# Zero fill moved from the front part into the experts, five warm-up transposes fewer, and maxima stored ahead of the due step

## The chip, the core and the metric

The kernel runs on one NeuronCore of a Trainium2 chip. Five engines work side by side, each through its own list of instructions in order: TensorE (PE in the profile; its weight loads are shown apart as PEld), VectorE (DVE), ScalarE (ACT), GpSimd (POOL) and SyncE (SP), which here issues most of the transfers (DMAs). Engines wait for one another through semaphores. PE reads SBUF and writes PSUM; PSUM has eight banks of 128 x 512 float32 values. The metric is the device time of one execution in microseconds, the median of several runs.

## The reference

A row of 2048 tokens with 448 features goes through two blocks, and a sigmoid gate mixes their outputs:

```python
g = sigmoid((x * gate_w).sum(-1, keepdims=True))
# A: attention, 16 heads of 28, no mask
q, k, v = split_heads(x @ wqkv)
p = softmax(q @ k.T * 28 ** -0.5)
a = merge_heads(p @ v) @ wo
# B: 8 experts of width 1792, the two best per token
logits = x @ w_gate
topk_idx = argsort(-logits)[:, :2]
gates = softmax(take_along_axis(logits, topk_idx))
for e in range(8):
    w = (gates * (topk_idx == e)).sum(-1, keepdims=True)
    b += w * (silu(x @ w1[e]) @ w2[e])
out = g * a + (1 - g) * b
```

Everything is float32. Outside attention's last products the kernel gets float32 accuracy by splitting each operand into a high part and a remainder, so that one product becomes two or three matmuls.

## The kernel before, in words

**Front part (lines 238 to 617).** First come `BUSY` transposes of an identity on PE (`pt<-ident`, L339), which produce nothing that is used. Then a loop over 16 blocks of 128 tokens makes the values `v`, the router's logits and the gate (`v_block`, L334). ACT copies the values of each block from PSUM into a tile `v_s` (L376, three buffers), DVE copies the logits (L377), and SP stores `v_s` to DRAM (`v_d`, L382). DVE and ACT split the next tokens and the q/k weights meanwhile. Then follow seven tiles of q and k for all tokens (`qk_tile`, L569). Between their matmuls DVE works through `routing()`, which finds each token's two experts and its slot; its first PE step is a matmul on the finished masks `mb` (L431), which depends on the logits of all 16 blocks.

Every expert has 640 slots in the DRAM tensor `ys_d`, of which up to 576 are filled, and 24 blocks of 128 slots stand behind them for tokens that do not fit. Slots that no expert writes must hold zeros. In the kernel before, SP stores them from the SBUF tile `zf` in the token loop, from block 4 on: 24 stores at L385 and 8 at L388, each 128 x 448 values.

**Experts (lines 672 to 950).** Each of 8 experts is worked in two halves of its width (`hf` 0 and 1); I number the 16 halves 0 to 15. A half first makes the hidden values: 7 pieces, each 2 x 11 matmuls of 288 columns, 154 in all (L870; called U matmuls). Then the second product: one small part for slots 513 to 576 under `tc.If(cnt > 512)` (`last_slots`, L800), then four blocks of 128 slots with 21 matmuls of 448 columns each, 84 in all (L920; Y matmuls). Two PSUM banks, `acc0` and `acc1`, serve U and Y in turn. In the second half of an expert the next expert's tokens are transposed in between (L722; these halves are called `turns` in the code).

**The stream of maxima (`max_stream`, L91).** The softmax of attention needs the largest score of each query, and these are found beside the experts. A cell is one product of 128 queries and 512 keys for one head (L106); there are 1024. A step issues six cells into the six banks `pm`, or seven, the first into the idle `acc` bank (`spare`), when that bank is free. DVE then reduces each cell to its maxima: the cell in `acc` at L120, the others at L126 in two instructions, and at L135 it folds 16 partial maxima into the tile `mg`. 64 cells make one unit (a group of four heads and 512 queries). With a unit's last cell, its `mg` is appended to the list `flush`. `store_max` (L141) takes one `mg`, transposes it on PE into the idle `acc` bank (L142), copies it on DVE (`mr`, L144) and stores it (`m_d`, L145).

**When a step or a store is issued.** The program calls `worked` after every U and Y matmul; the order of PE's instructions is fixed by it at build time, not on the chip. `w1_due` and `W2_DUE` list after which U or Y matmul a step becomes due (one more is due at the start of the Y matmuls). At a due place, `worked` issues a store if `flush` holds one and the idle bank may be used, and puts the step off for `STORE_NS` of PE work (three Y matmuls); otherwise it issues the step. The idle bank may be used between the due place and three matmuls behind it (`free`, L923).

The instructions of SP are ordered by the framework's scheduler, not by hand: it may issue a transfer far ahead of the place in the program where it is written, as soon as its data are there.

Of the kernel before, what the change touches and what calls it, by code (L numbers as in the profile page):

```python
# [8 lines left out]
F32 = mybir.dt.float32  # L9
# [8 lines left out]

NXT = 8
A_AT = (1, 4)  # L20
BUSY = 20
STORE_NS = 600
U_NS, Y_NS, YT_NS = 131, 206, 452

S, D, H, DH, E, FF = 2048, 448, 16, 28, 8, 1792
# [4 lines left out]
CPAD = 640  # L30
NMAIN = E * CPAD
# [18 lines left out]
def tile_gated_mha_moe(ctx: ExitStack, tc: tile.TileContext, x, xT, wv, wqk, wo, w1, w2, out):  # L50
    nc = tc.nc
# [3 lines left out]
    dram = ctx.enter_context(tc.tile_pool(name="dram", bufs=1, space=DRAM))  # L55
# [6 lines left out]
    sum_d = dram.tile([NG * 4, 4, 512], F32, name="sum_d")  # L62
    idx_d = dram.tile([128, NSP], I32, name="idx_d")
    ys_d = dram.tile([NS, D], F32, name="ys_d")

    ident = consts.tile([128, 128], F32, name="ident")
    coef = consts.tile([128, 3, NT], F32, name="coef")
# [73 lines left out]
    def store_max(g, qc, mg, bank):  # L141
        nc.tensor.transpose(bank[0:16, 0:128], mg.rearrange("p j t -> p (j t)"), ident)  # L142
        mr = mxp.tile([16, 128], F32R, name="mr")
        nc.vector.tensor_copy(mr, bank[0:16, 0:128])  # L144
        nc.sync.dma_start(m_d[4 * g + qc].rearrange("h (t q) -> (h t) q", q=128), mr.bitcast(F32))  # L145
        done.append((g, qc))

    flush = []
# [7 lines left out]
    def tail_twice(xt):  # L156
        nc.scalar.activation(xt[:, D:512], xt[:, 384:D], AF.Copy)
# [15 lines left out]
    want, hold = [0], [0]  # L173
# [10 lines left out]
    def worked(ns, due=False, bank=None):  # L184
        hold[0] = max(0, hold[0] - ns)
        want[0] += due
        if want[0] and not hold[0]:
            if flush and bank:
                store_max(*flush.pop(0), bank())
                hold[0] = STORE_NS  # L190
                return
            if bank:
                spare.append(bank())
            next(ms, None)
            want[0] -= 1
            spare.clear()
# [41 lines left out]
    with ExitStack() as pa:  # L238
# [65 lines left out]
        nc.gpsimd.dma_start(neg_d.rearrange("o (a n) -> o a n", a=4), bc(neg.unsqueeze(1), [1, 4, 512]))  # L304
        zf = sb.tile([128, D], F32, name="zf")
        nc.gpsimd.memset(zf, 0.0)
        sbase = sb.tile([128, E + 1], F32, name="sbase")
        nc.gpsimd.memset(sbase[:, 0:1], 0.0)
        mb = sb.tile([128, NT + 1, E], BF, name="mb")
# [45 lines left out]
        for t in range(NT):  # L355
            ts = slice(t * 128, (t + 1) * 128)
            if t != 1:
                for t_ in ((0, 1) if t == 0 else (t,)):
                    pvs[t_] = ps.tile([128, 512], F32, name="pq")[:, 0:NV]

                for t_, j in (((0, 0), (0, 1), (1, 0), (1, 1), (0, 2), (1, 2), (0, 3), (1, 3)) if t == 0 else
                              [(t, j) for j in range(4)]):
                    v_block(t_, j)
            pv = pvs.pop(t)
            if 0 < t and t + 2 < NT:
                split_xt(t + 2)
            if 4 <= t < 12:
                b, c = divmod(t - 4, 2)
                cs = slice(c * D, (c + 1) * D)
                nc.scalar.activation(wqk_h[:, b, cs], wqr[t - 4], AF.Copy)  # L370
                nc.vector.tensor_tensor(wqk_l[:, b, cs], wqr[t - 4], wqk_h[:, b, cs].bitcast(F32),
                                        op=ALU.subtract)
            v_s = wk.tile([128, H, 32], F32, name="v_s")
            nc.gpsimd.memset(v_s[:, :, DH:DH + 1], 1.0)
            nc.gpsimd.memset(v_s[:, :, DH + 1:32], 0.0)
            nc.scalar.activation(v_s[:, :, 0:DH], pv[:, 0:D].rearrange("p (h d) -> p h d", h=H), AF.Copy)  # L376
            nc.vector.tensor_copy(lg[:, t], pv[:, D:D + E + 1])  # L377
            if t + NXT - 1 < NT:
                load_x(t + NXT - 1)
            if t < 8:  # L380
                load_wq(t)
            nc.sync.dma_start(v_d[ts], v_s.rearrange("p h d -> p (h d)"))  # L382
            if t >= 4:
                for i in range(2 * t - 8, 2 * t - 6):
                    nc.sync.dma_start(ys_d[NMAIN + i * 128:NMAIN + (i + 1) * 128], zf)  # L385
                    if i % 3 == 0:
                        r0 = (i // 3 + 1) * CPAD
                        nc.sync.dma_start(ys_d[r0 - CPAD + 512:r0], zf)  # L388

        def tmp(name, shape, dt=F32):  # L390
            return sb.tile(shape, dt, name=name)
# [280 lines left out]
    with ExitStack() as pb:  # L672
# [45 lines left out]
        def turn_x(xg, k, xeh, xel):  # L718
            n = CT[k]
            pt = ps.tile([128, 512], F32, name=f"acc{turn[0] ^ 1}").rearrange("p (b n) -> p b n", b=4)  # L720
            for b in range(4):
                nc.tensor.transpose(pt[:, b, :n], xg[:n, b * 128:(b + 1) * 128], ident[:n, :n])  # L722
            h, l = xeh[:, :, k * 128:k * 128 + n], xel[:, :, k * 128:k * 128 + n]
            f = xf[:, k % 4].rearrange("p (b n) -> p b n", b=4)[:, :, :n]
            nc.scalar.activation(h, pt[:, :, :n], AF.Copy)
            nc.scalar.activation(f, pt[:, :, :n], AF.Copy)
            nc.gpsimd.tensor_tensor(l, f[:, 0:3], h[:, 0:3].bitcast(F32), op=ALU.subtract)
            nc.gpsimd.tensor_tensor(h[64:128, 3], f[64:128, 3], h[64:128, 3].bitcast(F32), op=ALU.subtract)
# [100 lines left out]
        w1_due = [(18, 46, 73, 100, 128), (11, 35, 59, 83, 107, 131)]  # L829


        W2_DUE = [(15, 13, 12, 10), (16, 14, 13, 12)]

        for e in range(E):
            cnt = nc.values_load(cnt_i[0:1, e:e + 1], min_val=0, max_val=S)
# [6 lines left out]
            for hf in range(2):  # L842
# [53 lines left out]
                for n_k, k in enumerate((4, 0, 1, 2, 3)):  # L896
                    if k == 4:
                        if hf == 0:
                            ysb[4] = sb.tile([128, D], F32, name="ysb", bufs=5)
                        if (e, hf) == (E - 1, 1):  # L900
                            spilled()

                            nc.scalar.activation(sb.tile([128, 1], F32, name="warm", bufs=1), ident[:, 0:1], AF.Exp)
                        with tc.If(cnt > 512):
                            last_slots(e, hf, hs, ysb[4])
                        worked(0, True)
                        for f in range(NH):
                            fetch_w2(base + f + 9)
                    n = CT[k]
                    cs = slice(k * 128, k * 128 + n)  # L910
                    turns = hf == 1 and e + 1 < E
                    due = W2_DUE[turns][n_k - 1]
                    if k < 4:
                        py = accumulator()
                    i = 0
                    for f in range(NH if k < 4 else 0):
                        hh, hl, ht = hs[f]
                        w2h, w2l, w2r = w2t[base + f]
                        for a, b in ((hh, w2h), (hh, w2l), (hl, w2h)):
                            nc.tensor.matmul(py[:n, 0:D], a[:, cs], b, start=i == 0, stop=i == 3 * NH - 1)  # L920
                            i += 1

                            free = due <= i < due + 4 and (n_k > 1 or not turns)  # L923
                            worked(Y_NS, i == due, other_accumulator if free else None)
                            if (e, hf, n_k) == (E - 1, 1, 4) and i in (1, 10):
                                first_scores(i == 10)
                        if hf == 1 and e + 1 < E and (f == 1 or f == 4 and n_k == 1):
                            j = n_k if f == 1 and n_k > 1 else f // 4
                            turn_x(xgs[j], j, xeh, xel)
                    if hf == 0:  # L930
                        if k < 4:
                            ysb[k] = sb.tile([128, D], F32, name="ysb", bufs=5)
                            nc.scalar.activation(ysb[k], py[:, 0:D], AF.Copy)
                        if e + 1 < E:
                            for j in {0: (0, 1), 4: ()}.get(n_k, (n_k + 1,)):
                                xgs.append(gather(e + 1, j))
                            for j in {0: (), 1: (0, 1)}.get(n_k, (n_k,)):
                                tail_twice(xgs[j][:CT[j]])
                    elif k < 4:
                        r0 = e * CPAD + k * 128  # L940
                        yo = sb.tile([128, D], F32, name="yo")
                        nc.scalar.activation(yo, py[:, 0:D], AF.Copy)
                        nc.gpsimd.tensor_tensor(yo, yo, ysb[k], op=ALU.add)
                        nc.sync.dma_start(ys_d[r0:r0 + n], yo)

                    free = {0: ((e * NP + 4, 0),), 1: ((e * NP + NP, 0), (e * NP + NP + 1, 2))}[hf]
                    for p, at in free:
                        if n_k == at:
                            split_w1_high(p, WHOLE)
                            split_w1_low(p, WHOLE)  # L950
# [207 lines left out]
```

## Time and profile before

| | us |
|---|---|
| median of 3 runs | 1443.89 (1442.52 to 1445.17) |
| the profiled execution | 1443.26 |
| its span in the profile | 1441.4 |
| PE busy | 1423.7 (99%) |
| ACT busy | 899.2 (62%) |
| DVE busy | 794.5 (55%) |
| POOL busy | 646.5 (45%) |
| bytes moved by DMAs | 153.18 MB, mean 106 GB/s |

The busy time of an engine is the union of its instructions' times; matmuls overlap, so that an instruction's duration is longer than the distance to the next one. In a row of the timeline the first number is the start in us from the span's start, the second the duration, then engine, line, operation, output <- inputs and shape; what stands in brackets is the engine's idle time before and what ended it.

### The profile page before, as it was taken

What the parts mean: (1) busy time and instruction counts of PE and PEld (TensorE: products, weight loads), DVE (VectorE), ACT (ScalarE), POOL (GpSimd) and SP (SyncE); (2) the same over time, 40 slices, a digit from 0 to 9 for tenths busy, and PEclk for the clock granted to TensorE, in tenths of its full rate; (3) what the DMA queues carried; (4) which work ended last, traced back from release to release, by engine and by line L of the source; (5) the groups of instructions that cost most, each with busy time, mean ns of one, the idle gap of its engine ahead of it and who ended that gap; (6) DMA issues with size and microseconds to landing.
All of it is one profiled execution on the core that took longest, in us unless ns stands there. A gap on an engine that the chain in (4) does not pass through costs nothing. (4 is left out here: it accounts for less than half of the span.)

```text
span 1441.4 us, 28118 instructions
## 1 busy us (share of the span) xinstructions
PE 1423.7 (99%) x11025; PEld 953.7 (66%) x11025; DVE 794.5 (55%) x858; ACT 899.2 (62%) x1559; POOL 646.5 (45%) x685
## 2 busy tenths in 40 slices
PE   9999999999999999999999999999999999999998
PEld 8788888888888888788888887533333333333347
DVE  5636777777778778778688787111142111221136
ACT  5235355344443553453444434799999999999981
POOL 1124597577666874874775656212222112112110
PEclk9999999999999999999999999999999999999999
DMA  9887532344133323331431320311422231142103
GB/s 332 291 289 238 169 112 78 97 136 129 43 103 118 103 81 110 123 98 55 137 118 37 107 70 3 108 47 49 130 55 59 78 98 47 43 122 64 32 20 119
DMA packets 110201, 153.18 MB, mean 106 GB/s; under 512 B 17884, under 2 KB 81516, under 8 KB 110064
## 3 DMA queue, kind: packets, MB, share of 16 engines
q1 hardware_dynamic: 100832, 129.86, 28.7%
q0 software_dynamic: 9088, 21.22, 4.9%
q8 instruction: 90, 1.47, 0.4%
q14 instruction: 47, 0.39, 0.1%
q10 hardware_dynamic: 144, 0.23, 0.1%
HBM read 109.20 MB, written 37.85 MB: 102 GB/s over the span
## 5 line engine op out<-in xcount | busy, mean ns | idle before, releaser
L126 DVE TENSOR_REDUCE mp<-pm 128x2 f32<-128x1024 f32 (+2 forms) x324 | 552.3, 1747 | 130.8 <-PE pm L106 130.3
L1058 ACT ACTIVATE P<-ps 128x1536 f32<-128x1536 f32 x254 | 367.9, 1448 | 0.0
L1067 PE MATMUL po<-P,V 128*32 128x512 f32 x2032 | 270.6, 604 | 0.0
L870 PE MATMUL acc<-xeh,w1l 128*128 128x288 f32 x880 | 258.5, 301 | 0.0
L870 PE MATMUL acc<-xeh,w1h 128*128 128x288 f32 x880 | 256.6, 298 | 0.0
L667 PEld LDWEIGHTS ps<-Q,Kh 29*128 29x128 f32 x2032 | 77.8, 183 | 212.6 <-ACT P L1057 212.3
L740 POOL TENSOR_TENSOR w2l<-w2r,w2h 128x448 fp32r<-128x448 f32 x112 | 129.0, 1153 | 168.9 <-ACT w2h L734 168.9
L870 PE MATMUL acc<-xel,w1h 128*128 128x288 f32 x660 | 195.1, 296 | 0.0
L667 PE MATMUL ps<-Q,Kh 29*128 29x512 f32 x2032 | 190.0, 444 | 0.0
L872 ACT ACTIVATE hh<-acc 128x288 fp32r<-128x288 f32 x224 | 92.3, 412 | 154.1 <-PE acc L870 154.1
L870 PEld LDWEIGHTS acc<-xeh,w1l 128*128 128x128 f32 x880 | 165.9, 189 | 18.6 <-issue 18.6
L920 PE MATMUL acc<-w2h,hh 128*128 128x448 f32 x448 | 171.8, 383 | 0.0
L870 PEld LDWEIGHTS acc<-xeh,w1h 128*128 128x128 f32 x880 | 165.7, 188 | 9.0 <-issue 7.3
L920 PE MATMUL acc<-w2l,hh 128*128 128x448 f32 x448 | 167.2, 373 | 0.0
L920 PE MATMUL acc<-w2h,hl 128*128 128x448 f32 x448 | 165.0, 368 | 0.0
L702 POOL TENSOR_TENSOR w1l<-w1r,w1h 128x512 fp32r<-128x512 f32 (+1 forms) x88 | 137.5, 1563 | 43.5 <-ACT w1h L696 25.3
L1071 DVE COPY osb<-po 128x512 f32<-128x512 f32 x16 | 11.1, 691 | 264.7 <-PE po L1067 246.9
L1014 POOL DMA_DIRECT2D sum_d<-osb x64 | 32.2, 515 | 271.7 <-DVE osb L1071 238.4
L1057 ACT ACTIVATE P<-ps 128x512 f32<-128x512 f32 x254 | 151.7, 597 | 1.4 <-ACT P L1058 0.5
L749 POOL TENSOR_TENSOR hl<-hf,hh 128x512 fp32r<-128x512 f32 x112 | 143.4, 1287 | 0.0
L106 PE MATMUL pm<-khg,qg 28*128 28x512 f32 x969 | 118.2, 454 | 9.7 <-DVE mp L126 5.9
L870 PEld LDWEIGHTS acc<-xel,w1h 128*128 128x128 f32 x660 | 124.6, 189 | 3.1 <-issue 2.9
(203 smaller groups left out, 1881.3 us busy)
## 6 DMA issues: line engine op xcount, KB each, us to landing
w2r<-in_w_dram SPq DMA_DIRECT2D x112, 224.0 KB
w1r<-in_w_dram SPq DMA_DIRECT2D x56, 384.0 KB
ys_d<-zf SPq DMA_DIRECT2D x32, 224.0 KB
qkh_d<-hi SPq DMA_DIRECT2D x28, 256.0 KB
qkl_d<-lo SPq DMA_DIRECT2D x28, 256.0 KB
w1r<-in_w_dram SPq DMA_DIRECT2D x112, 64.0 KB
ys_d<-yo SPq DMA_DIRECT2D x32, 224.0 KB
v_d<-v_s SPq DMA_DIRECT2D x16, 256.0 KB
```

The costliest lines, as they stand in the source:

```text
L106: nc.tensor.matmul(banks[n], qgs[g, qt // 4][rw, (qt % 4) * 128:(qt % 4 + 1) * 128], kh[g, kc][rw], start=True, stop=True)
L126: nc.vector.tensor_reduce(mp[:, (o + lo) % 256:(o + lo) % 256 + hi - lo], pm[:, lo:hi], axis=AX.X, op=ALU.max)
L667: nc.tensor.matmul(banks[j], k[rw, ks], q[rw, c], start=i == 0, stop=i == 2)
L702: nc.gpsimd.tensor_tensor(l[:, :, half], r[:, :, half], h[:, :, half].bitcast(F32), op=ALU.subtract)
L740: nc.gpsimd.tensor_tensor(w2l, w2r, w2h.bitcast(F32), op=ALU.subtract)
L749: nc.gpsimd.tensor_tensor(hl, hf32, hh[:, 0:512].bitcast(F32), op=ALU.subtract)
L870: nc.tensor.matmul(pu[:, 0:HC], a, b[:, cs], start=i == 0, stop=i == len(mms) - 1)
L872: nc.scalar.activation(hh[:, cs], pu[:, 0:HC], AF.Silu)
L920: nc.tensor.matmul(py[:n, 0:D], a[:, cs], b, start=i == 0, stop=i == 3 * NH - 1)
L1057: nc.scalar.activation(P[:, 0], p1, AF.Exp, scale=SCALE)
L1058: nc.scalar.activation(P[:, 1:4], p3, AF.Exp, scale=SCALE)
L1067: nc.tensor.matmul(po[32 * j:32 * j + 32], v[:, kt % 8, 32 * j:32 * j + 32], P[:, j] if n > 1 else P[j], start=kt == 0, stop=kt == NT - 1)
```

## The change

Four things are changed.

- The zeros go to DRAM once: a new tensor `zero_d` of 128 x 448 is stored from `zf` by POOL's queue. The 32 stores of `zf` in the token loop are gone. In their place stand 32 copies from `zero_d` to `ys_d`, DRAM to DRAM, written in the first half of each expert, one for each of the four blocks of slots.
- `BUSY` is 15 and was 20.
- `worked` issues a store whenever `flush` holds one, the bank may be used and nothing holds it back, whether a step is due or not; a step is issued only where no store is. The idle bank may now be used from Y matmul 10 of a block (12 in the `turns` halves) to three behind the due place.
- The due places of the steps in the four blocks of Y matmuls go from 15, 13, 12, 10 to 15, 14, 13, 12, and in the `turns` halves from 16, 14, 13, 12 to 16, 15, 14, 13.

```diff
-BUSY = 20
+BUSY = 15
...
+    zero_d = dram.tile([128, D], F32, name="zero_d")
...
     def worked(ns, due=False, bank=None):
         hold[0] = max(0, hold[0] - ns)
         want[0] += due
-        if want[0] and not hold[0]:
-            if flush and bank:
-                store_max(*flush.pop(0), bank())
-                hold[0] = STORE_NS
-                return
+        if not hold[0] and flush and bank:
+            store_max(*flush.pop(0), bank())
+            hold[0] = STORE_NS
+        elif want[0] and not hold[0]:
             if bank:
                 spare.append(bank())
             next(ms, None)
...
         nc.gpsimd.memset(zf, 0.0)
+        nc.gpsimd.dma_start(zero_d, zf)
...
             nc.sync.dma_start(v_d[ts], v_s.rearrange("p h d -> p (h d)"))
-            if t >= 4:
-                for i in range(2 * t - 8, 2 * t - 6):
-                    nc.sync.dma_start(ys_d[NMAIN + i * 128:NMAIN + (i + 1) * 128], zf)
-                    if i % 3 == 0:
-                        r0 = (i // 3 + 1) * CPAD
-                        nc.sync.dma_start(ys_d[r0 - CPAD + 512:r0], zf)
...
-        W2_DUE = [(15, 13, 12, 10), (16, 14, 13, 12)]
+        W2_DUE = [(15, 14, 13, 12), (16, 15, 14, 13)]
...
-                            free = due <= i < due + 4 and (n_k > 1 or not turns)
+                            free = (12 if turns else 10) <= i < due + 4 and (n_k > 1 or not turns)
                             worked(Y_NS, i == due, other_accumulator if free else None)
...
+                    if hf == 0 and n_k:
+
+                        r0 = e * CPAD + 512 if n_k == 1 else NMAIN + (3 * e + n_k - 2) * 128
+                        nc.sync.dma_start(ys_d[r0:r0 + 128], zero_d)
```

## The prediction

> **What bounds the kernel now.** I read the page first, then PE's waits over the whole span, then the timelines of PE, DVE, ACT and SP around each wait that the change touches.
>
> ```profile
> span 1441.4 us, 28118 instructions
> PE 1423.7 (99%) x11025; PEld 953.7 (66%) x11025; DVE 794.5 (55%) x858; ACT 899.2 (62%) x1559; POOL 646.5 (45%) x685
> ```
>
> PE is busy in all but 17.7 us of 1441.4 (other engines have large gaps), so a cut elsewhere counts only where PE waits, and every new wait of PE adds its full length. Its waits:
>
> ```profile
> engine line waited for: us in total, times, longest us
> PE pm L106 <- DVE mp L126: 5.9, 22, 0.6
> PE pt L431 <- DVE dl L424: 2.5, 1, 2.5
> PE pm L106 <- PEq L904: 2.2, 7, 0.4
> PE pt L339 <- DVE ident L266: 1.4, 1, 1.4
> ```
>
> Two of them are what the change can reach: 2.5 us in the front (L431) and 5.9 us in the experts, where a step of maxima finds DVE still reducing the step before it. So a gain of some 8 us is the most that could come of it.
>
> The sum is made against the profiled execution: 1443.26 us, its span and 1.9 around it. The median of the runs shown is 1443.89, 0.6 above; runs differ by about 0.2% (2.9 us), which is also what I call no change.
>
> **Part 1, the zeros.** The one long wait of the front and what leads to it (SP, ACT, DVE, PE):
>
> ```profile
> 12.06 0.34 SPq L385 DMA_DIRECT2D ys_d<-zf  x1
> ...
> 42.35 0.49 SPq L382 DMA_DIRECT2D v_d<-v_s  x1
> ...
> 44.08 0.54 ACT L376 ACTIVATE v_s<-pq 128x448 f32<-128x448 f32 x1 [1.82 <-DMA v_d<-v_s]
> 46.58 0.55 ACT L376 ACTIVATE v_s<-pq 128x448 f32<-128x448 f32 x1 [1.95 <-PE pq L569]
> ...
> 47.15 0.17 DVE L377 COPY lg<-pq 128x9 f32<-128x9 f32 x1 [2.33 <-ACT v_s L376]
> 51.46 0.29 DVE L422 TENSOR_TENSOR mb<-mask,mask 128x128 bf16<-128x128 f32 x1
> ...
> 49.04 0.39 PE L569 MATMUL pq<-xl,wqk_h 128*128 128x512 f32 x1
> 51.90 0.22 PE L431 MATMUL pt<-mb,tri 128*128 128x136 bf16 x1 [2.47 <-DVE dl L424]
> 52.83 0.40 PE L569 MATMUL pq<-xh,wqk_h 128*128 128x512 f32 x1
> 53.06 0.39 PE L569 MATMUL pq<-xl,wqk_h 128*128 128x512 f32 x1
> ```
>
> `v_s` has three buffers, so the last two copies of values (44.08, 46.58) wait until older `v_d` stores have landed (the row at 46.58 names PE, but PE had ended that block by about 44; the 13th store, issued at 42.35, is what frees its buffer). The logits follow, then 4.6 us of masks on DVE, and PE waits 2.47 us. The stores are late because the transfers are full:
>
> ```profile
> 22.00:44.00 22.00, 22.00 (x107) 19.81 (x106) 13.10 (x35) 11.94 (x24) 1.49 (x16) 1.00 0.99 351
> ...
> 120.00:915.00 795.00, 785.18 (x5201) 655.33 (x5199) 599.72 (x463) 360.22 (x946) 523.50 (x457) 1.00 0.32 101
> ```
>
> These rows are of the table by stretches; its last two columns are the share of the DMA engines and GB/s: 0.99 and 351 between 22 and 44 us. What takes the zeros' place there? The built order of SP in the changed kernel shows that the change does only half of what it says: the scheduler hoists 16 of the 32 copies from `zero_d` back among the `v_d` stores of the front, and the first three w1 tiles (512 KB each) with them; the other 16 go out early in experts 0 and 1. Up to and with the 13th `v_d` store I count, from the first zero store's place on, 44 transfers of 10,432 KB before (22 zero stores of 224 KB among them), and 37 of 8,384 KB after (six copies and 1,536 KB of w1). A fifth less at the same rate is about 6 us of the 30 between 12 and 42 us, more than the 2.6 by which the copy at 46.58 is late. Then the last logits are ready at about 44.7, when PE ends the block, the masks at 44.7 + 4.6 = 49.3, and PE, which arrives at 49.4, hardly waits. I take a gain of 2.4. Its bounds: 2.47, and nothing if copies from DRAM to DRAM, which no row shows, cost the engines half as much again per byte: two copies and a store per block of 2.27 us are 704 KB or 310 GB/s, under 351, but 409 GB/s with that surcharge. The store of `zero_d` on POOL's queue (224 KB at about 6 us) is 0.65 us of transfers, and I let the 1 us by which PE is behind its tokens there hide it. The 16 copies in the experts meet a DMA share of 0.32 between 120 and 915 us; SP's w1 loads behind them wait for POOL's buffers anyway. Cost 0, at most 1 us if a w2 tile comes late.
>
> **Part 2, the warm-up.**
>
> ```profile
> 1.41 4.53 PE L339 MATMUL pt<-ident 128*128 128x128 f32 x20 [1.41 <-DVE ident L266]
> 5.59 0.71 PE L334 MATMUL pq<-xeh,xh 128*128 128x458 f32 x1
> 6.58 0.47 PE L334 MATMUL pq<-xeh,xh 128*128 128x458 f32 x1
> ...
> 5.94 0.59 ACT L325 ACTIVATE xeh<-wv_r 128x458 fp32r<-128x458 f32 x1 [0.88 <-DMA wv_r<-in_wv_dram]
> ...
> 200.66 0.60 PE L722 MATMUL acc<-ident,xg 128*128 128x128 f32 x4
> ...
> 905.49 0.27 PE L142 MATMUL acc<-ident,mg 128*16 128x128 f32 x1
> ```
>
> Five transposes less let the first matmul (5.59) start about a us earlier, but the fourth (6.58) needs the weights that ACT has split at 5.94 + 0.59 = 6.53, after a load that nothing here moves. Gain 0. The warm-up's 20 transposes stand 0.21 us apart, (5.59 - 1.41) / 20; four of the same shape at 200.66 stand 0.11 apart, (0.60 - 0.27) / 3 with 0.27 for the last one's own time, as in the single transpose of the last row. So PE begins at half pace. If less early work prolongs that, some seven matmuls after 6.58 pay 0.2 us each: up to +1.5. I take 0.
>
> **Part 3, stores ahead of the due step.** This decides. One step of seven cells, two Y matmuls behind it, and DVE's last instruction of that step:
>
> ```profile
> 158.45 0.73 PE L106 MATMUL pm<-khg,qg 28*128 28x512 f32 x6
> 159.11 0.47 PE L920 MATMUL acc<-w2l,hh 128*128 128x448 f32 x1
> 159.42 0.36 PE L920 MATMUL acc<-w2h,hl 128*128 128x448 f32 x1
> ...
> 163.03 0.18 DVE L135 TENSOR_REDUCE mg<-mp 128x4 f32<-128x16 f32 x1
> ```
>
> A step occupies PE for 0.66 us, but its maxima are in `mg` only at 163.21, 4.76 us after its start. `flush` is filled while the step is issued, at build time, long before `mg` is there on the chip. Before, a store came only at the next due place, at least 17 Y matmuls later. Now `worked` issues the store at the very next Y matmul if the bank may be used, and after a due step it may for three more. The built order of PE confirms it. Of 16 stores, four stand at Y10 (halves 2, 4, 6, 8) and four at Y33 (3, 5, 7, 9), on units that an earlier step ended; but eight stand one Y matmul behind the very step that ends their unit: behind Y75 in halves 0, 10, 12, behind Y76 in 9 and 11, behind Y56 in 13, Y55 in 14, Y35 in 15. These eight alone wait for DVE, and for its newest count.
>
> PE gets there 0.97 us after the step's start (where 159.42 is), and `mg` is ready at 4.76. From DVE's end to PE's start pass 0.15 us (51.75 to 51.90 at L431), and 0.1 to load `mg` as weights: PE stands 4.76 + 0.25 - 0.97 = 4.04 us. Everything behind it on PE waits too, Y matmuls that need nothing of it included. Seven such stores: 7 x 4.05 = +28.4 (3.8 to 4.3 each: 26.6 to 30.1). Half 15's last step has four cells:
>
> ```profile
> 900.89 0.50 PE L106 MATMUL pm<-khg,qg 28*128 28x512 f32 x3
> 901.63 0.36 PE L920 MATMUL acc<-w2h,hl 128*128 128x448 f32 x1
> ...
> 903.80 0.18 DVE L135 TENSOR_REDUCE mg<-mp 128x4 f32<-128x16 f32 x1
> ```
>
> 903.98 + 0.25 - 901.63 = +2.6. ACT, POOL and the loads catch up meanwhile, but PE waited for none of them.
>
> The stores at Y10 change the place of a wait, not its size. In half 2 before:
>
> ```profile
> 251.79 0.27 DVE L144 CAST mr<-acc 16x128 fp32r<-16x128 f32 x1
> ...
> 252.21 0.50 PE L106 MATMUL acc<-khg,qg 28*128 28x512 f32 x1
> 256.31 0.49 PE L106 MATMUL acc<-khg,qg 28*128 28x512 f32 x1
> 256.91 0.73 PE L106 MATMUL pm<-khg,qg 28*128 28x512 f32 x6
> ```
>
> The copy `mr` queues on DVE behind the reductions of the step at Y0 and ends at 252.06; the step came at 252.21, after Y17, and the next found DVE busy for 0.60 us (256.31 to 256.91). After: the transpose goes out at Y10, `mr` still ends at about 252.06, and the step, due after Y15, needs the same bank: it starts at 252.2 too with three Y matmuls (0.61 us) less done. The next stands 20 instead of 16 Y matmuls on and waits for nothing: 0.61 lost, 0.60 gained, 0. Stores at Y33 find DVE free; 0. Halves 10 and 12 have no store ahead of Y15 any more; at most -0.2 each, and I take 0.
>
> **Part 4, later due places.** The last step moves by two Y matmuls (0.4 us) towards the next half's first. Only where six steps stand among the U matmuls (halves 9, 11, 13, 15) is that close:
>
> ```profile
> 559.49 0.73 PE L106 MATMUL pm<-khg,qg 28*128 28x512 f32 x6
> 560.62 3.41 DVE L126 TENSOR_REDUCE mp<-pm 128x3 f32<-128x1536 f32 x2
> ...
> 564.18 0.73 PE L106 MATMUL pm<-khg,qg 28*128 28x512 f32 x6
> ```
>
> DVE ends at 564.03 and PE comes at 564.18, with no slack. Half 9 pays +0.4 (DVE sets the pace through that half, so it is not won back); before 11 and 13 the new store has already emptied DVE; half 15 gains 0.2, since its step comes one matmul earlier.
>
> **The sum.** 28.4 + 2.6 + 0.4 - 0.2 - 2.4 = +28.8 on 1443.26: 1472.1, and I say 1472.
>
> **The rivals.**
> - PE's clock falls in the new waits. PE at half pace is in the rows of part 2. A wait that costs it the pace again adds half of some 4.2 us (1.41 to 5.59), 2.1: three of seven give 1478, all seven 1487. Against it: after the 2.47 us at L431 matmuls follow at full pace (52.83 to 53.06, 0.23 for 512 columns); 4 us no run shows. The Trainium skill, "TensorE: Matmul & The Clock Gate", section "HAM oscillation — how this bites in real kernels", has it that PE gaps over about 3.4 us halve the clock; by that rule all seven pay, about 1487. Its windows run free of the kernel, so a gap only a little longer need not hold a whole one.
> - The other side: matmuls overtake the waiting transpose. The place is the same eight stores; price: the 31.0 fall away, and 1441.1 is left. It decides if PE goes on with Y matmuls while `mg` is awaited. Against it: at 256.31 to 256.91 PE stood idle though Y matmuls behind the step needed nothing of DVE.
> - The front gains nothing, because of the copies from DRAM, or the warm-up costs 1.5: 1474.5 to 1476.
> - The waits are shorter, as `mg` is counted earlier than the step's end: at half the length 1457.
>
> **How the numbers follow.** Forecast 0.62; clock falls in several waits 0.15; front without gain 0.13; shorter waits 0.05; overtaking 0.04, all faster; 0.01 for a result within 0.2%. 1467 to 1482 holds the forecast (1469 to 1475 with its bounds), the front's rival and the clock's up to four waits: 0.83. The likeliest case's own range is 1469 to 1475. Slower 0.95, faster 0.04, same 0.01.
>
> **What would show it.** In PE's waits a new row: the weight load or transpose of L143 waiting for DVE's L136, eight times, longest 4.0, some 31 us together. The row of L431 gone or under 0.3. SP with 16 copies from `zero_d` ahead of the first `qkh_d` store. Y matmuls after the waits 0.20 us apart if the clock holds, 0.4 if not. First matmul at about 4.7, the fourth still near 6.6. The forecast is wrong if the eight stores show waits under 1 us, or if the maxima steps behind them lose waits that I have left standing.

## The result, and the profile after

The changed kernel takes 1482.14 us in the median of six runs (1481.06 to 1483.66), the kernel before 1444.2 beside it: a ratio of 1.0265, 95% interval 1.0252 to 1.0278, so 37.9 us more. The profiled execution took 1481.39 us, 38.1 more than that of before. The head of its page:

```profile
span 1479.5 us, 28102 instructions
PE 1434.1 (97%) x11020; PEld 962.4 (65%) x11020; DVE 794.3 (54%) x858; ACT 899.5 (61%) x1559; POOL 647.4 (44%) x686
```

PE's idle time grew from 17.7 to 45.4 us, that is by 27.7. But its busy time grew too, by 10.4, though it has the same work but for five transposes. So there are two losses: PE waits, and PE is slower. The waits of PE, longest in total first:

```profile
engine line waited for: us in total, times, longest us
PE acc L143 <- DVE mg L136: 27.6, 8, 3.7
PE pm L107 <- DVE mp L127: 6.3, 23, 0.8
PE pm L107 <- PEq L899: 2.1, 7, 0.3
PE acc L107 <- DVE mr L145: 2.0, 4, 0.6
```

The first row is new: the transposing matmul of a store (L142 before, L143 now) waits for the count `mg`, eight times. The row of L431, 2.5 us before, has gone.

Where the time lies shows in the first U matmul and the last Y matmul of the experts, in the timelines of PE before and after:

```profile
128.50 0.30 PE L870 MATMUL acc<-xeh,w1h 128*128 128x288 f32 x1
...
913.93 0.37 PE L920 MATMUL acc<-w2h,hl 128*128 128x448 f32 x1
```

```profile
125.86 0.30 PE L865 MATMUL acc<-xeh,w1h 128*128 128x288 f32 x1
...
952.19 0.37 PE L915 MATMUL acc<-w2h,hl 128*128 128x448 f32 x1
```

The front ends 2.64 us earlier. The experts take 826.33 us from the one row to the other, 785.43 before: +40.90. What follows takes 527.3 in place of 527.4. These three make the 38.1.

One early store and what follows it, half 0 in PE's timeline after:

```profile
165.90 0.49 PE L107 MATMUL acc<-khg,qg 28*128 28x512 f32 x1
165.91 0.73 PE L107 MATMUL pm<-khg,qg 28*128 28x512 f32 x6
166.57 0.47 PE L915 MATMUL acc<-w2h,hh 128*128 128x448 f32 x1
170.72 0.38 PE L143 MATMUL acc<-ident,mg 128*16 128x128 f32 x1 [3.69 <-DVE mg L136]
170.76 0.72 PE L915 MATMUL acc<-w2l,hh 128*128 128x448 f32 x1
171.28 0.57 PE L915 MATMUL acc<-w2h,hl 128*128 128x448 f32 x1
171.66 0.57 PE L915 MATMUL acc<-w2h,hh 128*128 128x448 f32 x1
172.03 0.57 PE L915 MATMUL acc<-w2l,hh 128*128 128x448 f32 x1
```

The Y matmul at 166.57 is the last before the store. A Y matmul takes 0.205 us of PE at full pace, so from 166.78 to 170.72 PE loses 3.94 us (the row's 3.69 counts from the end of its pipelined record). Then the Y matmuls stand 0.37 to 0.38 us apart in place of 0.20. The table by stretches says why; its columns are the stretch, its length, the busy times of PE, PEld, DVE, ACT and POOL, then the granted clock of PE and two columns on DMAs:

```profile
167.04:170.45 3.41, 0.00 (x0) 0.00 (x0) 3.41 (x3) 0.00 (x0) 0.00 (x0) 1.00 0.33 101
170.45:173.86 3.41, 3.14 (x9) 2.84 (x10) 0.46 (x3) 0.00 (x0) 0.00 (x0) 0.50 0.22 63
173.86:177.28 3.42, 3.42 (x27) 2.86 (x26) 0.02 (x1) 1.86 (x5) 0.49 (x1) 1.00 1.03 334
617.59:621.00 3.41, 1.05 (x6) 0.99 (x7) 2.55 (x4) 0.00 (x0) 0.00 (x0) 1.00 0.11 34
621.00:624.42 3.42, 3.42 (x15) 3.28 (x14) 0.00 (x0) 0.55 (x1) 1.14 (x1) 0.50 0.01 2
781.44:784.85 3.41, 0.73 (x8) 0.19 (x1) 3.28 (x3) 0.00 (x0) 0.00 (x0) 1.00 0.23 67
784.85:788.26 3.41, 2.53 (x8) 2.27 (x9) 1.10 (x3) 0.00 (x0) 0.00 (x0) 0.50 0.01 2
788.26:791.67 3.41, 3.41 (x15) 3.29 (x13) 0.00 (x0) 0.68 (x2) 0.00 (x0) 0.50 0.00 0
938.45:941.86 3.41, 1.76 (x10) 1.66 (x11) 1.84 (x3) 0.19 (x1) 0.00 (x0) 1.00 0.08 26
941.86:945.28 3.42, 3.42 (x19) 3.16 (x18) 0.00 (x0) 0.36 (x1) 1.15 (x1) 1.00 0.40 117
```

I set these stretches to where the recorded clock changes. It does so only on a grid of 3.41 us, which does not begin anew with a wait. A stretch in which PE stood idle for most of the time is followed by one at a clock of 0.50, and half 12's wait (781.44) by two. All seven long waits do this. Half 15's shorter one (938.45, PE busy for 1.76 of 3.41 us) does not. Summed over the seven places, PE is busy for 25.5 us at half clock (3.14, 3.42, 3.41, 3.29, 5.94, 3.41 and 2.94), which costs half of that, 12.8 us.

### The profile page after: what moved, and what is told of

The parts are those of the page before. It is cut to its first block, busy times and chain, and to the rows that moved or that the text cites. A ratio compares the mean times of both kernels' runs of the same rounds, so it can differ in the third digit from the quotient of the medians.

```text
span 1479.5 us, 28102 instructions
## 1 busy us (share of the span) xinstructions
PE 1434.1 (97%) x11020; PEld 962.4 (65%) x11020; DVE 794.3 (54%) x858; ACT 899.5 (61%) x1559; POOL 647.4 (44%) x686
## 5 line engine op out<-in xcount | busy, mean ns | idle before, releaser
L915 PE MATMUL acc<-w2h,hl 128*128 128x448 f32 x448 | 169.4, 378 | 0.0
L107 PE MATMUL pm<-khg,qg 28*128 28x512 f32 x969 | 118.2, 454 | 9.5 <-DVE mp L127 6.3
```

Source lines behind the costliest of these rows:

```text
L107: nc.tensor.matmul(banks[n], qgs[g, qt // 4][rw, (qt % 4) * 128:(qt % 4 + 1) * 128], kh[g, kc][rw], start=True, stop=True)
```

## The experiments

My theory, A: the whole loss comes from the eight stores that stand right behind their own step, by their waits and then by a stretch of half clock behind each of the seven long ones. Rival B: what the waits do not explain comes from elsewhere in the change (zero copies, due places, warm-up). Rival C: it comes from the idle time but grows with its length. Each set of four kernels ran beside runs of the kernel before on its own chip; a ratio is always against those. The first set stood beside 1444.41 us.

**The change without the early stores (old_enough).** On the changed kernel: the time of planned PE work since a unit's last step (`born`) and since the last step of any unit (`last`) is counted, and a store must wait until the first is 4.6 us and the second 3.4 us. Cuts are marked by dots:

```diff
+                        born[g, qt // 4] = clock[0]
...
+        clock[0] += ns
...
-        if not hold[0] and flush and bank:
+        if not hold[0] and flush and bank and clock[0] - born[flush[0][:2]] >= 4600 and (clock[0] - last[0] >= 3400 or len(done) == 15):
...
+            last[0] = clock[0]
```

> The changed kernel, but a store only when its unit's step lies 4.6 us of planned matmul time back and the last step 3.4 us (for the last unit the first condition alone), so none of the eight stands behind its own step; zeros, warm-up and due places stay as changed. Theory A (the eight early stores are the whole loss: their waits plus half clock behind them): no wait of L143's kind over 0.2 us, no stretch of half clock in the experts, and about 1440.5 us: 1444.2 less 2.4 of the front, and 1 to 2 us of the step waits gone, since the even halves' stores now fall well between two steps. Rival B (zero copies, later due places or the shorter warm-up make up the 8 to 10 us that the waits do not explain): 1449 to 1452.

Measured: 1441.31 us (1440.82 to 1442.28), ratio 0.998 (0.9971 to 0.9989). The first U and last Y matmul:

```profile
125.95 0.30 PE L869 MATMUL acc<-xeh,w1h 128*128 128x288 f32 x1
...
912.21 0.37 PE L919 MATMUL acc<-w2h,hl 128*128 128x448 f32 x1
```

The experts take 786.26 us, 40.07 less than after, without a stretch at half clock: the whole loss is gone, with zeros, due places and warm-up as changed. Theory A stands and B falls. The step waits, of which I expected 1 to 2 us to go, did not get shorter (6.4 us at L107, 5.9 before).

**The same waits with PE busy (filled, part_filled).** On the changed kernel, idle transposes stand ahead of the early stores' own. The edit is that of filled; part_filled has 20 and 10 of them in place of 33 and 20:

```diff
     def store_max(g, qc, mg, bank):
+        if clock[0] - born[g, qc] < 4600:
+            for _ in range(33 if len(done) < 15 else 20):
+                nc.tensor.transpose(bank[:, 0:128], ident, ident)
```

> The changed kernel, with 33 idle transposes of the identity (0.11 us each by the rows of the same shape, 3.6 us) put on TensorE ahead of each of the seven early stores, and 20 ahead of half 15's; the bank's result is overwritten by the store's own transpose. The waits stay as long in time, only TensorE is busy in them. Theory A (half clock, 3.4 us long, after a window in which TensorE stood idle): granted clock 1.00 from 7 us to the end, matmuls 0.20 apart behind the stores, and 1469 us, that is 1482.1 less 12.8 (the half-clock stretches of the profile with TensorE busy, halved). Rival B (the remainder does not come from idle time on TensorE): 1482 still.

> The same with 20 transposes in place of 33 (10 in half 15's), so some 1.7 us of each wait stay idle. Theory A, with a threshold (the clock falls only if a window of 3.4 us is more than about half idle; windows of the profile with 0.52 busy kept the clock, 0.31 did not): 1469 us too, clock 1.00. Rival C (what the idle time costs afterwards grows with its length): 1469 plus 1.7 / 3.9 of 12.8, 1474.5. Rival B: 1482.

Measured: filled 1471.56 us (1471.30 to 1471.83), ratio 1.0185 (1.0170 to 1.0201); part_filled 1470.44 (1470.10 to 1471.14), 1.0179 (1.0164 to 1.0195). The clock over the experts, filled:

```profile
120.00:943.00 823.00, 810.14 (x5431) 680.58 (x5429) 598.71 (x460) 359.45 (x945) 523.21 (x457) 1.00 0.33 100
```

Part_filled: its waits, the same stretch of the experts, and PE's timeline:

```profile
PE acc L147 <- DVE mg L136: 8.0, 8, 1.1
```

```profile
120.00:941.00 821.00, 800.13 (x5329) 668.62 (x5327) 598.71 (x460) 359.58 (x945) 523.26 (x457) 1.00 0.33 101
```

```profile
126.33 0.30 PE L871 MATMUL acc<-xeh,w1h 128*128 128x288 f32 x1
...
167.13 0.47 PE L921 MATMUL acc<-w2h,hh 128*128 128x448 f32 x1
167.75 2.40 PE L146 MATMUL acc<-ident 128*128 128x128 f32 x20
171.29 0.28 PE L147 MATMUL acc<-ident,mg 128*16 128x128 f32 x1 [1.14 <-DVE mg L136]
171.33 0.45 PE L921 MATMUL acc<-w2l,hh 128*128 128x448 f32 x1
171.62 0.36 PE L921 MATMUL acc<-w2h,hl 128*128 128x448 f32 x1
171.81 0.36 PE L921 MATMUL acc<-w2h,hh 128*128 128x448 f32 x1
...
940.90 0.37 PE L921 MATMUL acc<-w2h,hl 128*128 128x448 f32 x1
```

The store's transpose still comes 4.16 us after the last Y matmul (167.13 to 171.29), in the changed kernel 4.15 us (166.57 to 170.72). But the clock stays at 1.00 and the Y matmuls behind stand 0.20 apart. Work that produces nothing makes the kernel 11.7 us faster. The experts take 814.58 us: 11.75 less than after, which is what half clock costs, and 28.32 more than old_enough, which is about what the eight waits cost. The two kernels differ by 1.1 us the other way round from what more idle time would do: 33 transposes at 0.12 us (2.40 / 20) fill 4.0 us, a little more than the wait. The idle rest in part_filled was 1.1 us and not the 1.7 I had reckoned with, so this pair shows that 1.1 us of idle costs nothing afterwards, and not where the limit is.

**The new order of stores alone (stores_only).** The edits of `worked` and `free` on the kernel before:

```diff
-        if want[0] and not hold[0]:
-            if flush and bank:
-                store_max(*flush.pop(0), bank())
-                hold[0] = STORE_NS
-                return
+        if not hold[0] and flush and bank:
+            store_max(*flush.pop(0), bank())
+            hold[0] = STORE_NS
+        elif want[0] and not hold[0]:
...
-                            free = due <= i < due + 4 and (n_k > 1 or not turns)
+                            free = (12 if turns else 10) <= i < due + 4 and (n_k > 1 or not turns)
```

> The kernel before with only the new order of stores ahead of the due step (zeros, warm-up and due places as before). Theory A: the whole loss without the front's gain, 1444.2 + 38 + 2.4 = 1484.5. Rival B: the waits alone, 1444.2 + 29.7 = 1474.

Measured: 1485.27 us (1485.02 to 1486.75), ratio 1.0284 (1.0269 to 1.0300). Waits, and the experts' clock:

```profile
PE acc L142 <- DVE mg L135: 27.6, 8, 3.7
```

```profile
120.00:956.00 836.00, 797.76 (x5191) 666.35 (x5191) 599.94 (x463) 359.95 (x947) 523.19 (x457) 0.98 0.32 96
```

The same waits to the tenth, the same mean clock (0.98 in the experts of both), the whole loss; without the other edits the kernel is some 3 us slower than with them.

**The other edits alone (zeros_only, due_only).** The zeros' edit and the line of `W2_DUE` as in the change's diff, each on the kernel before. This set stood beside 1447.67 us. In all four of its profiles ScalarE and PE are held up once or twice, by 1 to 2.5 us, early in attention, and the stage behind the experts takes some 531 us, 527 in the other sets; so I read these four by their fronts and experts.

> The kernel before with the zeros' change alone. My account: the front's wait of 2.5 us before the transposing matmul of the counts goes, 1444.2 - 2.4 = 1441.8, and nothing changes in the experts. Rival: copies from DRAM to DRAM are so dear that the front gains nothing, or later copies hold up a tile of weights: 1444 or more.

> The kernel before with the later due places alone. My account: half 9's first step waits 0.4 us longer, half 11's and 13's as well now (no early store has emptied VectorE there), half 15's gains 0.2: 1444.2 + 1 = 1445.2, within what a measurement can tell. Rival (the due places carry part of the loss): over 1447.

Measured: zeros_only 1447.27 us (1445.43 to 1449.32), ratio 0.9994 (0.9984 to 1.0004); due_only 1447.54 (1446.39 to 1451.13), 1.0001 (0.9992 to 1.0011). The due places do nothing that can be told (experts 785.7 us). The zeros alone brought nothing that can be told either, where I expected 0.9983; the profile had a stretch of half clock in the front, so the same kernel stands once more below (zeros_again).

**One early store (one_early).** As old_enough, but the first store may go at once (the difference from old_enough):

```diff
-        if not hold[0] and flush and bank and clock[0] - born[flush[0][:2]] >= 4600 and (clock[0] - last[0] >= 3400 or len(done) == 15):
+        if not hold[0] and flush and bank and (not done or clock[0] - born[flush[0][:2]] >= 4600 and (clock[0] - last[0] >= 3400 or len(done) == 15)):
```

> The kernel old_enough with one early store left, that of half 0 (one transpose behind its own step). Theory A: 1441.3 plus a wait of 3.9 plus one stretch of half clock, 1.4 to 3.2 by where the free windows lie: 1446.6 to 1448.4. Without a fall of the clock: 1445.2. If only the many waits together brought the clock down: 1445.2 too.

Measured: 1450.95 us (1449.41 to 1453.09), ratio 1.0019 (1.0009 to 1.0030), where old_enough had 0.998: a difference of 0.0039, or 5.6 us. Over its own runs of before that is 3.3 us; theory A had 2.4 to 4.2 there, each of the two others 1.0. Its wait, and the stretches around it:

```profile
PE acc L144 <- DVE mg L136: 3.7, 1, 3.7
```

```profile
168.40:171.81 3.41, 0.91 (x5) 0.87 (x6) 2.69 (x4) 0.00 (x0) 0.00 (x0) 1.00 0.24 74
171.81:175.22 3.41, 3.41 (x13) 3.23 (x13) 0.00 (x0) 0.69 (x2) 0.00 (x0) 0.50 0.68 214
175.22:178.64 3.42, 3.42 (x27) 2.89 (x27) 1.08 (x1) 1.67 (x5) 1.14 (x1) 1.00 0.67 213
```

A single wait is enough. From its first U to its last Y matmul the experts take 791.51 us, 5.25 more than old_enough: 3.96 for the wait, and the other 1.3 are somewhat less than the 1.7 of a stretch at half clock.

**Longer waits (long_wait).** The changed kernel with two idle reductions on DVE ahead of the eight counts:

```diff
+                    if qt % 4 == 3 and 4 * g + qt // 4 in (0, 9, 10, 11, 12, 13, 14, 15):
+                        idle = mxp.tile([128, 4], F32, name="idle", bufs=1)
+                        for _ in range(2):
+                            nc.vector.tensor_reduce(idle[:, 0:3], pm[:, 0:3], axis=AX.X, op=ALU.max)
                     nc.vector.tensor_reduce(mg[:, :, qt % 4], part, axis=AX.X, op=ALU.max)
```

> The changed kernel with two more reductions of 1.71 us on VectorE (results unused) ahead of the count that each of the eight early stores waits for: waits of 7.3 us in place of 3.9, and 5.9 in half 15. Theory A (what the clock costs is the rest of one window of 3.4 us, or two, however long the wait was): 1482.1 + 8 x 3.42 + 1.6 for half 15, whose wait now fills a window too: 1511, give or take 4. Rival C (the price of the clock grows with the wait): 1520.

Measured: 1517.03 us (1516.96 to 1517.38), ratio 1.0477 (1.0458 to 1.0495). That is 69.4 over its own runs of before, where A had 66.8, give or take 4, and C 75.8. Waits, and half 13's stretches:

```profile
PE acc L147 <- DVE mg L140: 54.7, 8, 7.0
```

```profile
857.81:861.23 3.42, 0.84 (x3) 0.80 (x4) 2.77 (x4) 0.00 (x0) 0.00 (x0) 0.50 0.01 4
861.23:864.64 3.41, 3.41 (x10) 3.02 (x10) 0.00 (x0) 0.55 (x1) 0.86 (x1) 0.50 0.01 2
864.64:868.05 3.41, 3.41 (x22) 2.26 (x21) 0.56 (x1) 0.66 (x2) 1.19 (x3) 1.00 0.20 72
```

The waits grew by 27.1 us (54.7 - 27.6). PE's busy time at half clock in the experts is 36.6 us now, so half clock costs 18.3: 2.3 for each of eight waits, where it was 1.8 for each of seven. The wait had nearly doubled. So the price does not grow with the wait as C has it. The result lies within A's margin, but above its middle: PE often comes back in the middle of a stretch that is then mostly idle, and has to work through the next one at half clock too, as here.

**The front again (zeros_again, front_only, busy_only) and the best of both (old_enough_due).** Zeros alone, zeros with `BUSY = 15`, `BUSY = 15` alone, each on the kernel before; and old_enough with the old due places:

```diff
-BUSY = 20
+BUSY = 15
```

```diff
-        if not hold[0] and flush and bank and clock[0] - born[flush[0][:2]] >= 4600 and (clock[0] - last[0] >= 3400 or len(done) == 15):
+        if not hold[0] and flush and bank and clock[0] - born[flush[0][:2]] >= 4200 and (clock[0] - last[0] >= 3400 or len(done) == 15):
...
-        W2_DUE = [(15, 14, 13, 12), (16, 15, 14, 13)]
+        W2_DUE = [(15, 13, 12, 10), (16, 14, 13, 12)]
```

> The zeros' change alone, once more, since its first profile held a stretch of half clock in the front (22.6 to 26.0 us). My account: the first matmul of the experts at 126.0 in place of 128.5, experts as before (785.4 us), ratio 0.998. Rival (with the long warm-up the zeros gain nothing): first matmul of the experts at 128.5 or later without any stretch of half clock, ratio 1.000.

> The kernel before with the zeros' change and the shorter warm-up, stores and due places as before. My account: as the zeros alone, first matmul of the experts at 126.0, ratio 0.998. Rival: the shorter warm-up is what moves the front, 0.998 here and 1.000 for the zeros alone.

> The kernel before with the shorter warm-up alone. My account: nothing, first matmul of the experts at 128.5, ratio 1.000 (at most 1.001, if less early work keeps TensorE at half pace for seven matmuls more). Rival as in front_only: 0.998 to 0.999.

> The kernel old_enough with the due places of the kernel before (and 4.2 us as the age of a unit in place of 4.6). Its experts took 786.3 us against 785.4 before; if the later due places cost that 0.8 us, this has 785 us or a little less there (the stores stand well between two steps), the front's gain of 2.6, and a ratio of 0.9975. If the due places cost nothing: 0.998 as old_enough.

This set stood beside 1443.45 us.

| | median us | ratio (95%) | first U matmul | experts |
|---|---|---|---|---|
| zeros_again | 1442.32 | 0.9993 (0.9984 to 1.0002) | 127.33 | 786.3 |
| busy_only | 1442.85 | 0.9999 (0.9990 to 1.0008) | 127.72 | 785.5 |
| front_only | 1440.71 | 0.9982 (0.9973 to 0.9991) | 126.24 | 785.7 |
| old_enough_due | 1439.74 | 0.9976 (0.9967 to 0.9986) | 125.92 | 784.8 |

Neither the zeros nor the shorter warm-up alone brings a gain that can be told; together they do. That they need each other is not shown: 0.9993 times 0.9999 is 0.9992, and by the intervals the two small gains may simply add up. The profiles, one of each kernel, point the same way. The first U matmul starts at 128.50, 128.71 and 129.23 us where neither edit is made (before, due_only, stores_only), at 127.33 with the zeros alone (128.75 in the first run, with its stretch of half clock), at 127.72 with the shorter warm-up alone, and at 125.86 to 126.46 in the eight kernels that have both. The zeros alone take the wait for the masks away, as in the changed kernel, but another stands in PE's waits:

```profile
PE pq L336 <- ACT xh L161: 1.6, 1, 1.6
```

There PE waits until 21.95 us for tokens that ACT splits. With the shorter warm-up beside it that wait is 0.5 us, and in the changed kernel it is not listed. How five transposes at the start bear on a wait 20 us later I have not found out. In the profile of zeros_only the same wait (1.56 us, until 21.78) fell otherwise on the grid: PE was busy for 0.51 of one stretch, and half clock followed; in zeros_again it was busy for 0.67, and none did. In old_enough_due the experts take 784.8 us, 1.4 less than in old_enough and 0.6 less than before. It is faster than both kernels, than the one before by 0.24%: early due places, and stores that stand at least 17 Y matmuls behind a step, not one.

## Why the prediction was wrong

The direction was right (slower, given 0.95) and so was the mechanism: eight stores one Y matmul behind the step that ends their unit. The size was not: 1472 forecast, 1482.14 measured, just past the range's upper end of 1482. By the prediction's steps, against the profiled executions:

| step | predicted us | measured us |
|---|---|---|
| front, the wait for the masks | -2.4 | -2.64 to the first U matmul |
| eight stores' waits, half 9, half 15 | +31.2 | +29.15 (part_filled's experts against before) |
| clock in the new waits | 0 | +11.75 (after against part_filled) |
| after the experts | 0 | -0.13 |
| sum | +28.8 | +38.13 |

- **The failed step** is the clock. I left it out of the sum and gave it 0.15 as a rival, because matmuls follow at full pace behind the 2.47 us at L431. That row could not decide it. In the kernel before that wait fell across two stretches of the 3.41 us grid, with PE busy for 0.68 and 0.60 of them. What decides is whether one stretch is mostly empty, and a wait of 3.9 us nearly always leaves such a one: all seven did, where my range allowed for half clock behind four. The rival's price was 2.1 a wait (half of the 4.2 us at the start), which with all seven made 1487; it was 1.7 (11.75 / 7). The rule of the Trainium skill, "TensorE: Matmul & The Clock Gate", section "HAM oscillation — how this bites in real kernels", that idle gaps over about 3.4 us halve the clock, is what the trace shows at all seven places; by it I had worked out about 1487, 5 us too many. I had weighed it down by saying that a gap only a little longer need not hold a whole window. The rows show that the clock falls all the same: PE was busy for 1.05 of the 3.41 us ahead of 621.00, so no whole stretch was idle there, and half clock followed.
- **The waits** were 3.82 to 3.96 us (start of the store's transpose less that of the Y matmul before, less the 0.205 that this takes), in place of 4.05, and half 15's 2.52 in place of 2.6; eight make 29.7, not 31.0. The step and DVE took what I had said: `mg` was there at 170.67, 4.77 us after the step's start at 165.90. The hand-over that I had put at 0.25 was 0.05.
- **The zeros** did what the front's sum says, in the changed kernel:

```profile
6.70 0.48 PE L335 MATMUL pq<-xeh,xh 128*128 128x458 f32 x1 [0.67 <-ACT xeh L326]
...
38.51 0.53 SPq L383 DMA_DIRECT2D v_d<-v_s  x1
...
44.71 0.17 DVE L378 COPY lg<-pq 128x9 f32<-128x9 f32 x1 [2.12 <-ACT v_s L377]
...
49.46 0.22 PE L426 MATMUL pt<-mb,tri 128*128 128x136 bf16 x1
```

  The row at 38.51 is the 13th store of values, out 3.84 us earlier than before (42.35), so the copies from DRAM to DRAM ahead of it did not hold it up. The last logits are copied at 44.71 (44.7 foretold), and PE reaches the masks at 49.46 and does not wait (51.90 before). But I put the whole gain on the zeros and nothing on the warm-up, and the runs do not bear that out: with the zeros alone the first U matmul came 1.17 us earlier, not 2.4 (127.33 against 128.50). That the sum for the front came out nearly right is in part luck. The fourth matmul is at 6.70 (6.58 before), as foretold, and what the warm-up gives appears later.
- **Due places, stores at Y10 and Y33:** nothing measurable, as predicted (due_only 1.0001; the step waits 6.3 us in place of 5.9). The 2.0 us at `mr` are the four waits foretold for the stores at Y10, about half a us each, and the step behind them in half 2 no longer stops between its first cell and the others (both start at 259.72; 256.31 and 256.91 before). No run has the stores at Y10 and Y33 alone. The two other cheap rivals, overtaking and shorter waits, did not come: PE stood still for as long as DVE counted.

## What to carry to other kernels

When a new wait lands on TensorE that can leave 2 us or more of a 3.41 us stretch idle, price it at its length plus a stretch at half clock behind it (here 1.7 to 1.8 us, 2.3 where the wait was 7), and do not take a shorter wait's full pace behind it as evidence against that; the table by stretches with the granted clock decides it. An order that is fixed at build time must count the time until the result is there on the chip, not the moment at which its producer was issued; asking for 4.6 us of other planned work in between turned a loss of 2.65% into a gain of 0.2%, which comes from the front. If such a wait cannot be avoided, idle matmuls in it are cheaper than silence: here they gave back 11.7 of 38 us.

## What the runs showed of the hardware that I had not expected

- The granted clock changes on a grid of 3.41 us that is not tied to the program. Of the stretches at full clock in the 14 profiles, those in which PE was busy for 0.41 or less of the time (2.0 us of idle or more) were all followed by one at 0.50, those with 0.60 or more never; of the eleven in between three were, with 0.51, 0.52 and 0.58.
- A stretch at half clock in which PE idles again can be followed by another: half 12's was busy for 2.53 of 3.41 us at 0.50, and the next was at 0.50 again.
- Transposes by the identity count as work for this: 33 of them (or 20 with 1.1 us of silence) held the clock at 1.00.
- Whether a shorter wait brings half clock can depend on where it falls on the grid: one of about 1.6 us in the front did so in zeros_only (PE busy for 0.51 of one stretch) and not in zeros_again (0.67).
